# Cutting the opening weights of an MLP kernel into two rows by 131 KB and five rows by 328 KB

## The chip, the cores and the metric

The kernel runs on one core of a Trainium2 chip. The metric is the device time of one execution in microseconds; lower is better. The kernel before takes 398.3 us (the median of three executions, 397.71 to 398.58). Times inside an execution are counted from the start of the span that the profiler recorded.

## The reference

```python
y = _layernorm(x, axis=-1)                                  # x: 1 x 2048 x 1024, bf16
h = _gelu(jnp.einsum("bsd,df->bsf", y, w1) + b1)            # w1: 1024 x 3584
return jnp.einsum("bsf,fd->bsd", h, w2) + b2                # w2: 3584 x 1024
```

Each of the 2048 tokens is normalised over its 1024 channels, without gain or offset, then goes through a two-layer MLP with a hidden width of 3584 and the tanh form of GELU. All inputs and the output are bf16.

## The kernel before, in words

**Tiling.** Tokens come in 16 tiles of 128, and four tiles make a block of 512. The 1024 channels are 8 slices of 128 (`dt`), the 3584 hidden units are 28 rows of 128 (`r`). For each block the first product (`pe_row`, the matmul at L386) makes one row at a time: 8 matmuls of 128x128 weights against 512 tokens, summed in one PSUM bank, then GELU on ACT (L409). The second product (L451) takes all 28 rows of hidden units against w2, for 128 tokens and 512 output channels at a time; DVE adds b2 (L462) and SP stores.

**The opening.** The first block does not wait for whole weights. Its first seven rows (`R_WAVE = 7`, rows 0 to 6) are made in a wave of smaller matmuls, called cells here (`pe_wave`, L399), in an order that follows the loads:

1. Tiles 0 and 1 are turned by TensorE (`pe_T`, transposes at L342, copies out of PSUM by ACT at L358) as raw x, before they are normalised. Their cells run on raw values with 258 columns: 256 tokens and two columns of ones. DVE puts the normalisation in later, by subtracting the mean from the turned x (L511) for the rows to come and by fixing the seven rows in PSUM (L518, L521).
2. These 56 raw cells are ordered by `ROWS` (groups of rows), within a group by `QUARTERS` (two slices `dt` at a time), within a quarter by row and slice. With `ROWS = ((0, 1, 2, 3), (4, 5, 6))` a quarter of the first group is 8 cells, one of the second is 6.
3. After `T2_AT = 50` raw cells tile 2, which DVE and POOL have normalised by then (L255 statistics, L265, L262, L269), is turned into PSUM by eight transposes, and ACT copies it out.
4. Tile 2's 56 cells of 128 columns follow. After `T3_AT = 36` of them tile 3 is turned in the same way, then come the other 20, and then tile 3's own 56 cells, which wait for ACT's copy.
5. Rows 7 to 27 of block 0 follow as whole rows (L386).

Every engine works in its written order. PE therefore stands still at the first cell whose weights, tile or copy has not arrived, and everything behind that cell waits with it.

**The loads.** `dma` (L192) puts each load on SP's queue in a written order; each has its own semaphore. `SP_FIRST_LOADS` gives the first twelve: x0, x1, w0 to w3, x2, w4 to w7, x3 (b1 goes on ACT's queue). The rest of w1, the second block of x, w2, b2 and the last two blocks of x follow. `w0` to `w7` are entries of `w1_chunks`: each is a quarter (two slices `dt`) by 512 columns (four rows of hidden units), 256 rows of 1024 bytes in memory, 262 KB. w0 to w3 hold rows 0 to 3, w4 to w7 rows 4 to 7. w8 holds rows 8 to 11 with all slices, 1.05 MB in rows of 1024 bytes; w9 and w10 eight rows each in rows of 2048 bytes. A tile of x is 128 rows of 2048 bytes, also 262 KB. `pe_wave` and `pe_row` look up with `w1_chunk_of` which chunk a cell's weights are in, and wait for that chunk.

The functions that are touched follow.

Of the kernel before, what the change touches and what calls it, by code (L numbers as in the profile page):

```python
# [12 lines left out]
P = 128  # L13
# [10 lines left out]
GROUPS_0 = (0, 4, 8)  # L24
GROUPS_1 = (0, 8)
HALVES = (0, 4, 8)
ROWS = ((0, 1, 2, 3), (4, 5, 6))
QUARTERS = (0, 2, 4, 6, 8)
T2_AT = 50
T3_AT = 36  # L30
W1_EARLY = 2
W1_EARLY_COLS = 512
W1_COLS = (512, 1024, 1024)
N_W2_CHUNKS = 4
SP_FIRST_LOADS = ("x0", "x1", "w0", "w1", "w2", "w3", "x2", "w4", "w5", "w6", "w7", "x3")
ACT_FIRST_LOADS = ("b1",)
SLOT_0 = (1, 2, 3, 0)
N_ONES = 2
# [57 lines left out]
def bass_standalone__mixer_channel_mlp__prompt_kernel(  # L96
# [21 lines left out]
    R = R_WAVE  # L118
    assert R == NB1 + NB2 and R < FT
    assert NB1 + NB2 + 1 <= 8 and NB2 == 2  # L120
    assert all(c[-1] == DT for c in (GROUPS_0, GROUPS_1, HALVES))
    assert TPB == 4 and RAW == (0, 1) and sum(ROWS, ()) == tuple(range(R))

    w1_chunks = [(j0, j1, k * W1_EARLY_COLS, (k + 1) * W1_EARLY_COLS) for k in range(W1_EARLY)
                 for j0, j1 in zip(QUARTERS[:-1], QUARTERS[1:])]
    c0 = W1_EARLY * W1_EARLY_COLS
    for wdt in W1_COLS:
        w1_chunks.append((0, DT, c0, c0 + wdt))
        c0 += wdt
# [17 lines left out]
    with ExitStack() as es:  # L147
# [67 lines left out]
        def issue(item):  # L215
            if item == "b1":
                dma(b1r_sb[0:FT, :], b1.rearrange("(t p) -> t p", p=P), "b1", F * 2, waits=["b1z"])
            elif item[0] == "x":
                load_x_tile(int(item[1:]))
            elif item[0] == "w" and int(item[1:]) < len(w1_chunks):  # L220
                load_w1(int(item[1:]))
# [5 lines left out]
        dma_q[0] = sp  # L227
        for item in SP_FIRST_LOADS:
            issue(item)
# [312 lines left out]
        def wave_cell(r, dt, tiles, sig=None):  # L542
# [3 lines left out]

        cells = [(r, dt) for rows in ROWS for j0, j1 in zip(QUARTERS[:-1], QUARTERS[1:])
                 for r in rows for dt in range(j0, j1)]
# [5 lines left out]
        for j0, j1 in zip(HALVES[:-1], HALVES[1:]):  # L554
            for r in range(R):
                for dt in range(j0, j1):
                    if n == T3_AT:
                        pe_T(3, GROUPS_1, ("t",))
# [25 lines left out]
        for b in range(NB):  # L584
# [11 lines left out]
            for st in range(TPB):  # L596
                for dh in range(DH):
                    c0, c1 = dh * NCH, (dh + 1) * NCH
# [72 lines left out]
```

## Time and profile before

| | |
|---|---|
| median of three executions | 398.3 us (397.71 to 398.58) |
| the profiled execution | 398.81 us |
| its span | 397.6 us |
| the chain that ended last | PE 95% of the span |
| the first cell (L399) | at 6.2 us |
| tile 2's turn, tile 3's turn | at 12.2 and 15.9 us |
| the first whole row (L386) | at 20.8 us |
| DMA, 40 slices of 9.9 us | 252, 375, 387, 387, 387, 145 GB/s, then mostly under 30 |
| load to landing, eight pieces of 256 KB | median 5.5 us |

The profiled execution is 1.2 us longer than its span, which is the part outside of the recorded instructions. PE is the engine of all matmuls and PEld the weight loads that run ahead of them; DVE, ACT, POOL and SP are the vector, scalar, general-purpose and synchronising engines. A timeline line gives the start and the length in us, the engine, the line of the kernel and the operation with its output and input; the count at its end says how many were merged. Square brackets give the idle time of the engine just before and what ended it. In a chain of work that ended last each piece was released by the one above it. In a table by stretches the last two numbers are the mean busy share of the 16 DMA engines and what they moved in GB/s.

### The profile page before, as it was taken

The page shows a single profiled execution, that of the slowest core. Times are in us where ns is not written, and L with a number is a line of the kernel's source. Part 1 is how long each engine was busy: PE and PEld are TensorE (multiplying, and loading weights), DVE is VectorE, ACT ScalarE, POOL GpSimd, SP SyncE. Part 2 cuts the span into 40 slices and gives each one's busy share as a digit, 9 for nine tenths or more (in the row PEclk, how much of TensorE's full clock was granted, in tenths as well). Part 3 has the DMA queues.
Part 4 walks back from the last instruction along what each step waited for, and adds up shares of the span by engine and source line. Part 5 has one row for each costly group of instructions (what it writes and reads, how often), then busy time and mean ns, then how long its engine had stood idle before and what let it go on. Part 6 is the DMA issues. An engine that isn't in the chain of part 4 may idle for free.

```text
span 397.6 us, 4718 instructions
## 1 busy us (share of the span) xinstructions
PE 391.5 (98%) x2015; PEld 189.7 (48%) x2050; DVE 154.3 (39%) x335; ACT 82.7 (21%) x124; POOL 10.6 (3%) x56
## 2 busy tenths in 40 slices
PE   8999999999999999999999999999999999999998
PEld 7844444444444444444444444444444444444446
DVE  5759898989999005988100000001100000001111
ACT  3264430000134432000024433100003334400000
POOL 2101000020001000000000000000000000000000
DMA  7999930000000000000000000000000000000001
GB/s 252 375 387 387 387 145 15 26 26 16 26 1 2 0 0 2 26 14 28 26 15 0 0 2 0 12 16 26 13 28 13 2 0 0 2 13 26 15 26 28
DMA packets 16350, 23.64 MB, mean 59 GB/s; under 512 B 1482, under 2 KB 8522, under 8 KB 16330
## 3 DMA queue, kind: packets, MB, share of 16 engines
q1 hardware_dynamic: 16288, 23.33, 16.7%
q8 instruction: 16, 0.26, 0.3%
q14 instruction: 4, 0.03, 0.0%
q10 hardware_dynamic: 42, 0.01, 0.0%
HBM read 19.14 MB, written 4.19 MB: 59 GB/s over the span
## 4 chain that ended last, share of the span: by engine, by line
PE 95%; DMA 2%; SPq 1%; issue 1%; DVE 1%; POOL 0%
PE ps L451 48%; PE ps L386 45%; DMA x_sb<-in_x_dram 2%; SPq L192 1%; PE ps L399 1%; DVE st_sb L255 0%; PE ps_t L342 0%; POOL rstd_sb L262 0%; DVE x_sb L269 0%; DVE o_sb L462 0%; DVE mv_sb L265 0%
## 5 line engine op out<-in xcount | busy, mean ns | idle before, releaser
L451 PE MATMUL ps<-w_sb,hT_sb 128*128 128x512 bf16 (+1 forms) x964 | 193.4, 360 | 0.8
L386 PE MATMUL ps<-yT_sb,w_sb 128*128 128x512 bf16 x821 | 180.8, 379 | 1.0
L451 PEld LDWEIGHTS ps<-w_sb,hT_sb 128*128 128x128 bf16 x980 | 91.3, 98 | 102.6
L409 ACT ACTIVATE hT_sb<-ps,b_sb 128x512 bf16<-128x512 f32 x112 | 76.8, 688 | 253.2 <-PE ps L386 231.8
L386 PEld LDWEIGHTS ps<-yT_sb,w_sb 128*128 128x128 bf16 x840 | 82.1, 98 | 98.9
L462 DVE TENSOR_TENSOR o_sb<-ps,b_sb 128x512 bf16<-128x512 f32 (+1 forms) x35 | 22.6, 646 | 198.9 <-PE ps L451 198.9
L312 DVE STREAM_TRANSPOSE yT_sb<-x_sb 32x256 bf16<-32x256 bf16 x192 | 83.7, 436 | 26.4 <-PE ps L386 23.3
L255 DVE BATCH_NORM_STATS2 st_sb<-x_sb 128x6 f32<-128x512 bf16 x32 | 20.9, 671 | 7.3 <-DMA x_sb<-in_x_dram 7.3
L399 PE MATMUL ps<-yT_sb,w_sb 128*128 128x128 bf16 (+1 forms) x168 | 13.4, 237 | 1.4 <-DMA w_sb<-in_w_dram 1.4
L399 PEld LDWEIGHTS ps<-yT_sb,w_sb 128*128 128x128 bf16 x168 | 11.4, 98 | 3.1 <-DMA w_sb<-in_w_dram 2.2
L262 POOL TENSOR_TENSOR rstd_sb<-mv_sb,nhalf 128x1 f32<-128x1 f32 x14 | 7.7, 549 | 115.0 <-DVE mv_sb L265 115.0
L425 DVE TENSOR_TENSOR ps<-ps,row_r 128x256 f32<-128x256 f32 x21 | 8.9, 427 | 4.7 <-PE ps L386 4.7
L269 DVE TENSOR_SCALAR x_sb<-x_sb,mv_sb,rstd_sb 128x1024 bf16<-128x1024 bf16 x14 | 7.6, 544 | 3.3 <-POOL rstd_sb L262 2.7
L473 PE MATMUL ps<-const-bfloat16-1.0 128*128 128x128 bf16 x30 | 3.4, 300 | 0.8 <-PEq L656 0.8
L473 PEld LDWEIGHTS ps<-const-bfloat16-1.0 128*128 128x128 bf16 x30 | 3.0, 139 | 0.8 <-issue 0.8
L518 DVE SCALAR_TENSOR_TENSOR ps<-row_r,ncs,ps 128x256 f32<-128x256 f32 x7 | 3.4, 480 | 0.0
L265 DVE BATCH_NORM_AGGREGATE mv_sb<-st_sb 128x2 f32<-128x15 f32 x14 | 3.1, 222 | 0.4
L358 ACT COPY yT_sb<-ps_t 128x512 int32<-128x512 int32 (+1 forms) x3 | 1.5, 516 | 7.7 <-PE ps_t L342 7.7
L521 DVE TENSOR_TENSOR ps<-ps,row_r 128x256 f32<-128x256 f32 x7 | 3.0, 432 | 0.2
L490 ACT COPY row_r<-row_r 32x512 f32<-32x512 f32 x3 | 1.9, 617 | 3.2 <-DVE row_r L484 3.2
L511 DVE TENSOR_TENSOR yT_sb<-yT_sb,row_r 128x1024 bf16<-128x1024 bf16 x2 | 2.4, 1216 | 0.0
L342 PE MATMUL ps_t<-ident,x_sb 128*128 128x128 bf16 x20 | 1.7, 226 | 0.1
(21 smaller groups left out, 12.5 us busy)
## 6 DMA issues: line engine op xcount, KB each, us to landing
w_sb<-in_w_dram SPq DMA_DIRECT2D x4, 1792.0 KB, 18.3
w_sb<-in_w_dram SPq DMA_DIRECT2D x2, 2048.0 KB, 15.9
out_dram<-o_sb SPq DMA_DIRECT2D x31, 128.0 KB, 1.7
x_sb<-in_x_dram SPq DMA_DIRECT2D x3, 1024.0 KB, 14.3
w_sb<-in_w_dram SPq DMA_DIRECT2D x8, 256.0 KB, 5.5
x_sb<-in_x_dram SPq DMA_DIRECT2D x4, 256.0 KB, 4.2
w_sb<-in_w_dram SPq DMA_DIRECT2D x1, 1024.0 KB, 9.0
b_sb<-in_b_dram SPq DMA_DIRECT2D x1, 256.0 KB, 14.3
```

Source lines behind the costliest of these rows:

```text
L192: dma_q[0].op(lambda e, dst=dst, src=src: e.dma_start(dst, src), waits=waits, sig=sig, sem="d_" + sig, inc=16)
L255: return (lambda e, i=i, h=h, pw=pw: e.bn_stats(st_sb[i][:, 6 * h:6 * (h + 1)], x_sb[:, i, h * pw:(h + 1) * pw]), [x_ev[i][h if len(x_ev[i ...
L262: pool.op(lambda e, i=i, dst=dst, mv=mv: e.tensor_tensor(out=dst, in0=mv[:, 1:2], in1=nhalf[:, i:i + 1], op=ALU.pow), waits=[f"mv{i}", "nh ...
L269: return (lambda e, i=i, c0=c0, c1=c1: e.tensor_scalar(out=x_sb[:, i, c0:c1], in0=x_sb[:, i, c0:c1], scalar1=mv_sb[:, i, 0:1], scalar2=rst ...
L312: res.append((lambda e, src=src, dst=dst: e.transpose(out=dst, in_=src), waits, (f"tr{i}" if lastop else None), 0.47))
L386: pe.op(lambda e, b=b, r=r, dt=dt, bank=bank: e.matmul(unit_bank(bank)[:, 0:TB], lhsT=w1_sb[:, dt, r * P:(r + 1) * P], rhs=yT_sb[:, b % 2, ...
L399: pe.op(lambda e: e.matmul(unit_bank(bank)[:, n0:n1], lhsT=w1_sb[:, dt, r * P:(r + 1) * P], rhs=yT_sb[:, 0, dt, n0:n1], start=(dt == 0 and ...
L409: act.op(lambda e, r=r, n0=n0, n1=n1, bank=bank: e.activation(out=hT_sb[:, r, n0:n1], in_=unit_bank(bank)[:, n0:n1], func=ACT.Gelu_apprx_tanh,
L425: crit.append((est[sig], (lambda e, reg=reg: e.tensor_tensor(out=reg, in0=reg, in1=row_b(1), op=ALU.mult), [sig, "row_r"], ready, 0.45), 0))
L451: pe.op(lambda e, sl=sl, ft=ft, c0=c0, c1=c1, bank=bank: e.matmul(ps_2[:, bank, 0:c1 - c0], lhsT=hT_sb[:, ft, sl * P:(sl + 1) * P], rhs=w2 ...
L462: crit.append((est[sig], (lambda e, ob=ob, c0=c0, c1=c1, bank=bank: e.tensor_tensor(out=o_sb[:, ob, c0:c1], in0=ps_2[:, bank, 0:c1 - c0], ...
L473: pe.op(lambda e: e.matmul(ps_1[:, 0, 0:P], lhsT=ones, rhs=ones, start=True, stop=True))
```

## The change

The same weights are loaded in other pieces, and the raw cells are grouped to match. w0 to w3 hold rows 0 and 1 only: a quarter by 256 columns, 256 rows of 512 bytes, 131 KB each. w4 to w7 hold rows 2 to 6: a quarter by 640 columns, 256 rows of 1280 bytes, 328 KB each. w8 becomes 640 columns, rows 7 to 11, 1.31 MB in rows of 1280 bytes, and w9 and w10 stay. The raw cells come in the groups (0, 1) and (2 to 6), so a quarter of the first group is 4 cells and one of the second 10. x2 is issued behind w5 instead of behind w3. Tile 3 is turned after 44 cells of tile 2 instead of 36, which leaves 12 of them behind it. The number of loads and of matmuls stays as it is.

```diff
-ROWS = ((0, 1, 2, 3), (4, 5, 6))
+ROWS = ((0, 1), (2, 3, 4, 5, 6))
 QUARTERS = (0, 2, 4, 6, 8)
 T2_AT = 50
-T3_AT = 36
-W1_EARLY = 2
-W1_EARLY_COLS = 512
-W1_COLS = (512, 1024, 1024)
+T3_AT = 44
+W1_COLS = (640, 1024, 1024)
 N_W2_CHUNKS = 4
-SP_FIRST_LOADS = ("x0", "x1", "w0", "w1", "w2", "w3", "x2", "w4", "w5", "w6", "w7", "x3")
+SP_FIRST_LOADS = ("x0", "x1", "w0", "w1", "w2", "w3", "w4", "w5", "x2", "w6", "w7", "x3")
...
-    w1_chunks = [(j0, j1, k * W1_EARLY_COLS, (k + 1) * W1_EARLY_COLS) for k in range(W1_EARLY)
+    w1_chunks = [(j0, j1, rows[0] * P, (rows[-1] + 1) * P) for rows in ROWS
                  for j0, j1 in zip(QUARTERS[:-1], QUARTERS[1:])]
-    c0 = W1_EARLY * W1_EARLY_COLS
+    c0 = R * P
```

## The prediction

> **What bounds the kernel now.** I read the page first (span and the busy shares), then the chain that ended last, cut to its first 25 us, because the change touches nothing behind the opening; then the timeline of the opening, and last the stretches with their DMA rates. The page:
>
> ```profile
> span 397.6 us, 4718 instructions
> PE 391.5 (98%) x2015; PEld 189.7 (48%) x2050; DVE 154.3 (39%) x335; ACT 82.7 (21%) x124; POOL 10.6 (3%) x56
> ```
>
> PE is busy from end to end, so a microsecond is won or lost only where the opening moves the first full 512-column matmul (L386). The chain, start and length in us, shows what sets that moment:
>
> ```profile
> 6.36 6.71 DMA x_sb<-in_x_dram
> 13.09 1.30 DVE st_sb L255 x2
> ...
> 15.30 0.56 DVE x_sb L269
> 15.90 0.62 PE ps_t L342 x8
> 16.52 4.24 PE ps L399 x76
> ...
> 20.82 4.26 PE ps L386 x19
> ```
>
> Tile 3 of x lands at 13.09, is normalised by 15.86, turned by eight transposes from 15.90, and 76 cells of 128 columns follow with no hole. But the margin by which x3 is last is thin. In the timeline (start, length, engine, work; in brackets the idle time before and what ended it):
>
> ```profile
> 6.20 3.42 PEld L399 LDWEIGHTS ps<-yT_sb,w_sb 128*128 128x128 bf16 x32 [1.30 <-DMA w_sb<-in_w_dram]
> 9.01 1.28 DVE L255 BATCH_NORM_STATS2 st_sb<-x_sb 128x6 f32<-128x512 bf16 x2 [0.49 <-DMA x_sb<-in_x_dram]
> 10.16 0.55 PEld L399 LDWEIGHTS ps<-yT_sb,w_sb 128*128 128x128 bf16 x6 [0.54 <-DMA w_sb<-in_w_dram]
> 10.91 0.55 PEld L399 LDWEIGHTS ps<-yT_sb,w_sb 128*128 128x128 bf16 x6 [0.20 <-DMA w_sb<-in_w_dram]
> 11.67 0.55 PEld L399 LDWEIGHTS ps<-yT_sb,w_sb 128*128 128x128 bf16 x6 [0.20 <-DMA w_sb<-in_w_dram]
> 12.23 0.54 PEld L342 LDWEIGHTS ps_t<-ident,x_sb 128*128 128x128 bf16 x8
> 13.62 2.01 PEld L399 LDWEIGHTS ps<-yT_sb,w_sb 128*128 128x128 bf16 x36 [0.30 <-ACT yT_sb L358]
> 15.89 0.45 PEld L342 LDWEIGHTS ps_t<-ident,x_sb 128*128 128x128 bf16 x8 [0.26 <-DVE x_sb L269]
> 16.30 4.28 PEld L399 LDWEIGHTS ps<-yT_sb,w_sb 128*128 128x128 bf16 x76
> ```
>
> PE opens on w0 at 6.20, waits for w4, w5 and w6 (10.16, 10.91, 11.67), turns tile 2 at 12.23, runs 36 cells of tile 2 and then waits 0.26 us for tile 3. So the weights' landings set tile 2's turn, and tile 3's landing wins over that chain by only 0.26 us. The stretches (length, busy time of PE, PEld, DVE, ACT, POOL, then granted clock, DMA share, GB/s):
>
> ```profile
> 3.40:4.50 1.10, 1.10 (x17) 1.00 (x15) 1.08 (x2) 0.33 (x2) 0.00 (x0) 1.00 0.80 194
> 4.50:6.20 1.70, 0.58 (x11) 0.40 (x8) 1.70 (x6) 0.87 (x4) 0.10 (x1) 1.00 0.95 318
> 6.20:8.30 2.10, 2.09 (x19) 1.88 (x20) 1.77 (x9) 0.00 (x0) 0.97 (x2) 1.00 1.02 322
> 13.20:14.20 1.00, 0.98 (x15) 0.69 (x14) 1.00 (x2) 0.37 (x1) 0.00 (x0) 1.00 1.11 351
> 20.00:30.00 10.00, 9.95 (x57) 4.91 (x56) 5.56 (x14) 6.62 (x10) 0.00 (x0) 1.00 1.05 387
> ```
>
> Between 13.2 and 14.2 only w8 moves (rows of 1 KB), from 20 on only rows of 2 KB: that prices a row. At 3.4 to 4.5, where x gives way to the weights, the rate is only 194, and it stays at 318 to 322 up to 8.3.
>
> **The price of a row.** 351 GB/s on 16 DMA engines is 21.9 each, 46.7 ns for 1 KB; 387 is 24.2 each, 84.7 ns for 2 KB. A line through both: 8.7 ns a row and 38.0 ns for 1024 bytes. So 512 bytes cost 27.7 ns, 1280 bytes 56.2. Every one of the eight pieces keeps 256 rows, 16 for each engine: 0.75 us for the old pieces (the waits above end 0.75 and 0.76 apart, as they should), 0.44 for the new w0 to w3, 0.90 for the new w4 to w7. No row of 512 bytes is in the trace. From below it can't beat the line by more than the 8.7 ns (bytes alone, 19 ns); from above it costs as much as the 1 KB row, 46.7. I take the line, since it also fits the 1 KB rows' 0.75 us in the opening; the upper end is the first rival. The Trainium skill ("DMA: Bandwidth & Descriptors", section "Why small descriptors are slow (HBM only)") gives three cycles of overhead beside 32-byte beats, so 19 cycles for 512 bytes against 35 for 1 KB and 43 for 1280. As an estimate from that page the rows take 25.3 and 57.4 ns, tile 2's turn comes 0.09 us sooner than below and the sum is 398.4; no run here shows a row of that size yet.
>
> **The landings.** w0 to w3 lose 0.305 us each, 1.22 together; w4 to w7 gain 0.152 each. Times before are the releases above.
> - w0: 6.20 - 0.30 = 5.90. PE is free for it: its three filler matmuls start at 4.75 and ACT's last copy of tile 1 ends at 5.37.
> - x2 moves behind w4 and w5: 9.01 - 1.22 + 2 x 0.90 = 9.59. On SP it is issued two places later (each issue takes 0.43 to 0.60 us), at about 4.7 instead of 3.71, nearly 5 us ahead of its landing, so the issue hides under the queue; w4 and w5 go out two and one places sooner, w6, w7 and x3 where they were.
> - w6: 11.65 - 1.22 + 3 x 0.152 = 10.89. w7 (issued at 5.85, 6.5 us to landing, 12.4): 12.4 - 1.22 + 0.61 = 11.8. x3: 13.09 - 0.61 = 12.48.
> - w8 grows by 0.26 MB, just what the eight pieces lose (row 7 moves over). Its 64 rows per engine cost 0.61 more, so it lands where it did, at 7.04 + 9.0 = 16.0; row 7 needs it at 20.8. Without that cover of 4.8 us each late microsecond would count in full. Later chunks and w2 are unmoved.
>
> **PE.** A 258-column cell takes 0.11 us (w0's 32 cells ran in 3.5 us without a hole), a 128-column one 0.0559 (76 in 4.25). Rows 0 and 1 are 4 cells a piece, rows 2 to 6 are 10. w0 to w3: 5.90 to 7.66 (w3 lands at 7.0). w4 lands at 7.9, its cells run to 9.0; w5's to 10.1; then a wait for w6, 10.9 to 12.0; four cells of w7 to 12.45, where tile 2's turn stands (after 50 cells in both kernels). Tile 2's y comes 2.76 us behind its landing (13.09 to 15.85 in tile 3's row; the same DVE, POOL, DVE steps): 9.59 + 2.76 = 12.35. So tile 2 is turned at 12.45 instead of 12.23: PE starts 0.3 us sooner but gets there no sooner, because w4 to w6 and x2 all have to land first. The 1.39 us from the turn to the first tile 2 cell (12.23 to 13.62; six RAW cells and ACT's copy) stay. The 44 cells ahead of tile 3's turn take 2.46: 12.45 + 1.39 + 2.46 = 16.30. Tile 3's y is there at 12.48 + 2.81 = 15.29, a microsecond early, so the wait of 0.26 is gone, and x3's gain is lost on PE's backlog. Behind the turn (0.41) stand now only 12 cells (0.67) instead of 20 (1.12) to cover the copy, which releases tile 3's cells 1.30 behind the turn (15.89 to 17.19: copy at 16.56, 0.59 long): a new wait of 0.22, on which all of PE is queued. Then 56 cells, 3.13. End: 16.30 + 1.30 + 3.13 = 20.73 against 16.30 + 4.25 = 20.55 before: **0.18 us later**. DVE's centring of tiles 0 and 1 follows tile 3's y, so it ends earlier than its 18.11 and hides; so do its fixes, which follow tile 3's cells.
>
> **Sum.** Profiled execution 398.81 (span 397.6 and 1.2 around it) + 0.18 = 398.99. It stands 0.51 above the median of 398.3, so 398.5 for the median.
>
> **Rivals.**
> - *The small rows cost as much as the old ones* (slower). w0 to w3 then gain nothing and w4 to w7 cost 0.152 each: w6 lands at 12.11, tile 2 is turned at 13.66, the end is 1.21 later than forecast: 399.7. It decides (0.8 us over before) from 37 ns a row: (0.8 - 0.18) / 64 rows = 9.7 ns over 27.7. For it: the four pieces move just in the stretch where the engines are at 194 to 322 GB/s, so rows and their latency limit there, not bytes. Against it: the steady line. The Trainium skill (same page, section "Measured (HBM→SBUF, 128 partitions, SWDGE, issued from GpSimd)") has a rule against such pieces: batch to 1 MiB, small transfers go by descriptors. The 256 KB pieces ran at 91% of the best rate here, which speaks against it; for 131 KB nothing does yet.
> - *The slow start shrinks with the pieces* (faster). x1 lands at 1.22 + 3.0 = 4.2 and w0 at 6.20: 2.0 us for a piece worth 0.75. I left the excess of 1.2 in place. If all of it went, w6 and x2 would land 1.2 sooner, tile 2 would be turned at about 11.25 and PE reach tile 3's turn at 15.1 with y3 at 14.1: end 19.53, 397.3. Over half a microsecond more than half of that excess must go (0.98 us) for a gain of 0.8. Against it: the DMA count and rows are the same, and the gap lies at the change from x to weights, which stays.
> - *x3 still decides*, as the chain has it now, with the 0.61 us that it gains: turn at 15.29, end 15.29 + 1.30 + 3.13 = 19.72, 397.5. It needs tile 2's turn by 11.44, a microsecond sooner than worked out.
>
> **How the numbers follow.** About 0.2% (0.8 us) is what a measurement of this kernel can tell from no change. Forecast, within that: 0.50. Small rows dear, or stalls of the start that cost more with x2 queued behind six pieces: 0.36. The two faster ones: 0.14 together, since both need the slow start to shrink. The unshown row price and the stall are far larger than my 0.18. The range runs from 397.7 (a part of the excess gone) to 399.8 (small rows at the old price); the forecast's own range is 397.9 to 399.0.
>
> **What would show it.** PE's first cell at 5.9; waits for weights ahead of the fifth and the seventh piece; tile 2's statistics at 9.6 instead of 9.01; its turn at 12.45; no wait ahead of tile 3's turn at 16.3, but one of 0.2 for ACT's copy behind it; the first L386 matmul at 21.0 (20.82 + 0.18). The forecast is wrong if tile 2's turn lies outside 11.5 to 13.1, or if row 7 waits for w8.

## The result

The change makes the kernel slower. The median over seven executions is 399.44 us (399.12 to 400.67) against 398.37 us for the kernel before; the ratio is 1.0033, with a 95% interval of 1.0020 to 1.0045, so about 1.1 to 1.3 us. That lies in the forecast range, at its slower end. But the likeliest case, a shift within 0.2%, did not come.

The profiled execution of the kernel after took 400.67 us, 1.2 us over its own median, so it is not a typical one. The page:

```profile
span 399.2 us, 4753 instructions
PE 394.2 (99%) x2050; PEld 190.4 (48%) x2050; DVE 154.3 (39%) x335; ACT 82.8 (21%) x124; POOL 10.6 (3%) x56
```

PE is still the bound, and the span is 1.6 us longer. The chain that ended last, cut to the opening (start, length, work):

```profile
4.73 6.38 DMA x_sb<-in_x_dram
11.13 1.30 DVE st_sb L253 x2
...
13.34 0.56 DVE x_sb L267
13.95 0.62 PE ps_t L340 x8
14.57 0.66 PE ps L397 x6
15.24 2.63 PE ps L397 x44
17.88 0.46 PE ps_t L340 x8
18.36 0.59 ACT yT_sb L356
...
19.08 3.30 PE ps L397 x56
22.38 2.81 PE ps L384 x13
```

Line numbers are two lower than before. The x tile at its head is now x2 (issued at 4.73), not x3: tile 2 lands at 11.1, is turned at 13.95, and everything behind is PE's own work plus ACT's copy behind tile 3's turn. Weight loads of the same opening in the timeline (start, length, engine, work, idle time before and what ended it):

```profile
5.80 1.67 PEld L397 LDWEIGHTS ps<-yT_sb,w_sb 128*128 128x128 bf16 x16 [0.18 <-issue]
9.62 2.09 PEld L397 LDWEIGHTS ps<-yT_sb,w_sb 128*128 128x128 bf16 x20 [2.15 <-DMA w_sb<-in_w_dram]
12.05 1.43 PEld L397 LDWEIGHTS ps<-yT_sb,w_sb 128*128 128x128 bf16 x14 [0.34 <-DMA w_sb<-in_w_dram]
13.94 0.45 PEld L340 LDWEIGHTS ps_t<-ident,x_sb 128*128 128x128 bf16 x8 [0.46 <-DVE x_sb L267]
15.24 2.46 PEld L397 LDWEIGHTS ps<-yT_sb,w_sb 128*128 128x128 bf16 x44 [0.30 <-ACT yT_sb L356]
17.66 0.49 PEld L340 LDWEIGHTS ps_t<-ident,x_sb 128*128 128x128 bf16 x8
19.07 3.13 PEld L397 LDWEIGHTS ps<-yT_sb,w_sb 128*128 128x128 bf16 x56 [0.26 <-ACT ncs L562]
```

PE begins on time (5.80, worked out as 5.90) and finishes the 16 cells of rows 0 and 1. Then it stands still for 2.15 us: w4 comes at 9.62, and I had worked out 7.9. The stretch from 4.5 to 9.1 us shows that the loads come more slowly. The kernel before (length, busy times of PE, PEld, DVE, ACT, POOL, granted clock, DMA share, GB/s):

```profile
4.50:9.10 4.60, 3.47 (x38) 2.98 (x36) 3.78 (x15) 1.42 (x5) 1.07 (x2) 1.00 1.00 324
```

The same stretch of the kernel after:

```profile
4.50:9.10 4.60, 3.22 (x30) 2.61 (x27) 3.89 (x14) 1.69 (x5) 1.07 (x2) 1.00 0.95 288
```

The opening moves 36 GB/s less. The experiments ask why. "Over before" is always the ratio with its interval, times 398.5 us.

### The profile page after: what moved, and what is told of

It is laid out like the page before. It is cut to its first block, busy times and chain, and to the rows that moved or that the text cites. A ratio compares the mean times of both kernels' runs of the same rounds, so it can differ in the third digit from the quotient of the medians.

```text
span 399.2 us, 4753 instructions
## 1 busy us (share of the span) xinstructions
PE 394.2 (99%) x2050; PEld 190.4 (48%) x2050; DVE 154.3 (39%) x335; ACT 82.8 (21%) x124; POOL 10.6 (3%) x56
## 4 chain that ended last, share of the span: by engine, by line
PE 96%; DMA 2%; SPq 1%; DVE 1%; issue 0%; ACT 0%; POOL 0%
PE ps L449 49%; PE ps L384 45%; PE ps L397 2%; DMA x_sb<-in_x_dram 2%; SPq L190 1%; DVE st_sb L253 0%; PE ps_t L340 0%; ACT yT_sb L356 0%; POOL rstd_sb L260 0%; DVE x_sb L267 0%; DVE o_sb L460 0%; DVE mv_sb L263 0%; ACT ncs L562 0%
```

## Experiments: which part of the change costs

**The cut alone.** The kernel after, with x2 and tile 3's turn put back:

```diff
-T3_AT = 44
+T3_AT = 36
-SP_FIRST_LOADS = ("x0", "x1", "w0", "w1", "w2", "w3", "w4", "w5", "x2", "w6", "w7", "x3")
+SP_FIRST_LOADS = ("x0", "x1", "w0", "w1", "w2", "w3", "x2", "w4", "w5", "w6", "w7", "x3")
```

> Edit: the kernel after with x2 back behind w3 and tile 3's turn back after 36 cells, so only the cut of the weights differs from before. Theory A (the cut costs: w4 to w6 land later than the thinner w0 to w3 give back, PE stands still for them): most of the 1.07 us stays, 0.5 to 1.1 us over before. Theory B (x2 behind w5 is the cost: its statistics start late and tile 2's turn waits for its y): about 0, within 0.3 us of before. Theory C (tile 3's turn is too late and the copy behind it is uncovered): 0.25 us less than the kernel after.

Measured: ratio 1.0033 (1.0019 to 1.0047), 1.3 us over before: all of the loss, even a little above what theory A gave. Its weight loads in the timeline:

```profile
6.74 0.78 PEld L397 LDWEIGHTS ps<-yT_sb,w_sb 128*128 128x128 bf16 x8 [0.45 <-DMA w_sb<-in_w_dram]
9.57 3.63 PEld L397 LDWEIGHTS ps<-yT_sb,w_sb 128*128 128x128 bf16 x34 [2.05 <-DMA w_sb<-in_w_dram]
13.22 0.54 PEld L340 LDWEIGHTS ps_t<-ident,x_sb 128*128 128x128 bf16 x8
```

PE waits 0.45 us within rows 0 and 1, and then 2.05 us for w4. From 9.57 on it runs 34 cells of 0.107 us without a hole, and tile 2's turn is late because PE is. x2 was ready long before. So theory A holds for the part, though not yet for the reason. Theories B and C are not needed for the loss: it is all there without x2's and tile 3's move.

**x2 alone.** The kernel before with x2 behind w5:

```diff
-SP_FIRST_LOADS = ("x0", "x1", "w0", "w1", "w2", "w3", "x2", "w4", "w5", "w6", "w7", "x3")
+SP_FIRST_LOADS = ("x0", "x1", "w0", "w1", "w2", "w3", "w4", "w5", "x2", "w6", "w7", "x3")
```

> Edit: the kernel before with x2 behind w5 and nothing else. Two pieces of 0.75 us ahead of it put x2 at about 10.5 instead of 9.01, its y at 13.3, and tile 2's turn from 12.23 to 13.3. Theory B: 0.8 us over before (13.3 + 1.39 + 2.01 + 0.41 + 4.25 = 21.36 against 20.55). Theory A: x2 is not what decides, w6 is; under 0.3 us over before.

Measured: ratio 1.0028 (1.0017 to 1.0038), 1.1 us over before. The timeline:

```profile
6.31 5.61 PEld L399 LDWEIGHTS ps<-yT_sb,w_sb 128*128 128x128 bf16 x50 [0.69 <-DMA w_sb<-in_w_dram]
10.48 1.29 DVE L255 BATCH_NORM_STATS2 st_sb<-x_sb 128x6 f32<-128x512 bf16 x2 [1.97 <-DMA x_sb<-in_x_dram]
13.29 0.45 PEld L342 LDWEIGHTS ps_t<-ident,x_sb 128*128 128x128 bf16 x8 [1.37 <-DVE x_sb L269]
```

All as theory B worked it out (x2 at 10.5, the turn at 13.3), and a little dearer in time. So moving x2 is bad by itself too, but the two costs do not add: together with the cut they give 1.0031 to 1.0033, no more than the cut alone. Tile 2's turn waits for the later of PE's backlog and tile 2's y, and in the change both are late.

**Tile 3's turn alone.** The kernel before with `T3_AT = 44`:

> Edit: the kernel before with tile 3's turn after 44 cells instead of 36. By theories A and B the wait of 0.26 us ahead of the turn goes and one of 0.22 behind it comes: within 0.1 us of before. Theory C: 0.2 us or more over before.

Measured: ratio 1.0001 (0.9992 to 1.0010). As worked out, one wait replaces another: in its profile PE waits for nothing ahead of the turn and 0.26 us behind it, where before it waited 0.26 ahead. Theory C falls.

**The kernel after again**, with a profile of its own:

> The kernel after unchanged, with a profile of its own. In the first profile w4 lands at 9.6 us though 7.9 was worked out. If that is one late DMA engine by chance (theory D), w4's release moves by over half a microsecond from profile to profile and the time with it; if it belongs to the pieces of 1280-byte rows (theory A), PE's second wait ends near 9.6 again. The time: 1.0 to 1.1 us over before in both cases.

Measured: ratio 1.0031 (1.0021 to 1.0040). Its weight loads:

```profile
5.77 1.67 PEld L397 LDWEIGHTS ps<-yT_sb,w_sb 128*128 128x128 bf16 x16 [0.41 <-issue]
8.22 0.99 PEld L397 LDWEIGHTS ps<-yT_sb,w_sb 128*128 128x128 bf16 x10 [0.78 <-DMA w_sb<-in_w_dram]
9.90 0.99 PEld L397 LDWEIGHTS ps<-yT_sb,w_sb 128*128 128x128 bf16 x10 [0.69 <-DMA w_sb<-in_w_dram]
11.45 1.44 PEld L397 LDWEIGHTS ps<-yT_sb,w_sb 128*128 128x128 bf16 x14 [0.56 <-DMA w_sb<-in_w_dram]
13.38 0.45 PEld L340 LDWEIGHTS ps_t<-ident,x_sb 128*128 128x128 bf16 x8 [0.50 <-DVE x_sb L267]
```

w4 came 1.4 us sooner than in the first profile (8.22), so that much was chance, as theory D has it. The trace holds a landing for each of the 16 DMA engines: in the first profile 15 of them had brought their share of w4 by 7.30 and the last one at 9.57, and PE waited for that one. But it is still later than 7.9, w6 is 0.56 late (10.89 worked out), and tile 2's turn stands at 13.38 instead of 12.45: 0.93 late, where the time is about 1 us late. The rate from 4.5 to 9.1 is 281 GB/s here and 282 in the run of the cut alone. Something systematic remains.

## Experiments: why the cut pieces come slowly

**Other cuts.** Three groupings ask whether the length of the rows does it. In the first two the cut is by `ROWS`, with x2 and tile 3's turn as before:

```diff
-ROWS = ((0, 1), (2, 3, 4, 5, 6))
+ROWS = ((0, 1, 2), (3, 4, 5, 6))
...
```

> Edit: the cut alone (x2 behind w3, tile 3's turn after 36 cells), but rows 0 to 2 in w0 to w3 (768-byte rows) and rows 3 to 6 in w4 to w7 (1024-byte rows). Theory P (a row costs its steady price from the start, only profiles by chance showed stalls): w6 0.6 us sooner, tile 3's turn 0.35 us sooner than before: 0.35 us under before. Theory S (in the first 9 us the engines don't reach the steady rate with the shorter rows, so thin first pieces gain little, and the fuller second pieces hand PE more cells behind w6): between before and the cut (2, 5), 0.2 to 0.9 us over before.

Measured: ratio 1.0002 (0.9993 to 1.0011). Neither theory: worse than P's 0.35 us under before, better than S's 0.2 us over. The rate from 4.5 to 9.1 is 337 GB/s, so the pieces of 197 KB do not have the trouble of those of 131 KB.

```diff
-ROWS = ((0, 1), (2, 3, 4, 5, 6))
+ROWS = ((0, 1, 2, 3), (4, 5, 6))
...
```

> Edit: rows 0 to 3 in w0 to w3 as before, rows 4 to 6 in w4 to w7 (768-byte rows, 197 KB), row 7 moves to w8; x2 and tile 3's turn as before. This takes from the cut only that row 7 is no longer loaded ahead of x3. Theory P: w4 to w7 land 0.15 us sooner each, x3 0.61: 0.6 us under before. Theory S: the first pieces are as before, the short rows come between 8 and 11 us where the rate is nearly steady: 0.3 to 0.6 us under before. If any row under 1 KB is dear (theory R, 47 ns a row whatever its length): no gain, within 0.1 us of before.

Measured: ratio 0.9993 (0.9984 to 1.0002): 0.3 us under before by the middle, not clear of no change. In its profile x3 comes about a microsecond sooner than in the profile of before (12.11 against 13.09). Short rows late in the opening do no harm, which speaks against theory R but doesn't refute it.

In the third, the kernel before gets the 1280-byte rows only in w4 to w7:

```diff
-W1_EARLY = 2
-W1_EARLY_COLS = 512
-W1_COLS = (512, 1024, 1024)
+W1_EARLY_COLS = ((0, 512), (512, 1152))
+W1_COLS = (384, 1024, 1024)
...
```

> Edit: the kernel before with w4 to w7 at 640 columns (1280-byte rows, rows 4 to 8) and w8 at 384; the cells and their order stay. Theory P and theory S: w4 to w7 land 0.15 us later each, x3 0.61 later, tile 3's turn waits for it: 0.6 us over before. Theory L (it is the 1280-byte rows that stall an engine): another 0.7 us or more, 1.3 us over before, and a spread of the landings of one piece over the 16 engines of 1.2 us and more.

Measured: ratio 1.0019 (1.0010 to 1.0028), 0.8 us over before, where P and S gave 0.6 and L 1.3. The interval still reaches 1.1 us, but the rate does not fall:

```profile
4.50:9.10 4.60, 4.60 (x43) 4.04 (x41) 4.24 (x16) 1.49 (x5) 1.08 (x2) 1.00 1.07 366
```

The extra bytes ahead of x3 cost what they should, within the interval. The rows of 1280 bytes stall nothing here: the 16 engines land a piece of them within 0.8 us of each other, where theory L asked for 1.2 and more. Theory L falls.

**The pace of the issues.** SP puts out one load in about 0.5 us, whether it is of 131, 262 or 328 KB: with 131 KB pieces that is 257 GB/s. Two edits of the cut alone keep all rows and bytes and change only the issuing. The cut alone moves in the stretch from 4.5 to 9.1:

```profile
4.50:9.10 4.60, 2.75 (x28) 1.89 (x25) 4.25 (x16) 1.63 (x5) 1.07 (x2) 1.00 0.90 282
```

In the first edit, two pieces go by ACT's queue:

```diff
-SP_FIRST_LOADS = ("x0", "x1", "w0", "w1", "w2", "w3", "x2", "w4", "w5", "w6", "w7", "x3")
-ACT_FIRST_LOADS = ("b1",)
+SP_FIRST_LOADS = ("x0", "x1", "w0", "w2", "x2", "w4", "w5", "w6", "w7", "x3")
+ACT_FIRST_LOADS = ("b1", "w1", "w3")
```

> Edit: the cut alone with w1 and w3 issued on ACT's queue (behind b1) instead of SP's, so everything behind them is issued up to 1 us sooner. Theory I (the pieces are too small for SP's pace of one issue in 0.51 us, 257 GB/s with 131 KB, and engines run dry): the rate between 4.5 and 6.2 us rises to 300 GB/s and more, and the time falls by 0.5 us or more against the cut alone. Theory S without the pace: within 0.2 us of the cut alone, 1.1 to 1.5 us over before.

Measured: ratio 1.0012 (1.0003 to 1.0021), 0.5 us over before and 0.8 under the cut alone, although w0 now shares the engines with w1 and PE opens only at 6.52. From 4.5 to 6.2 the rate is 300 GB/s, as theory I asked for; from 4.5 to 9.1:

```profile
4.50:9.10 4.60, 3.47 (x31) 2.71 (x30) 4.24 (x15) 1.75 (x5) 1.07 (x2) 1.00 1.03 336
```

In the second, rows 0 and 1 come in two pieces of four slices, two issues fewer with the same 512-byte rows (`SP_FIRST_LOADS` names the pieces anew in the same order, which is left out):

```diff
-                 for j0, j1 in zip(QUARTERS[:-1], QUARTERS[1:])]
+                 for j0, j1 in zip(*((HALVES[:-1], HALVES[1:]) if rows == ROWS[0] else (QUARTERS[:-1], QUARTERS[1:])))]
...
```

> Edit: the cut alone with rows 0 and 1 in two pieces of four slices (262 KB, 512 rows of 512 bytes) instead of four of two slices; the same rows and bytes by two issues fewer. Theory I (SP's pace of one issue in 0.51 us feeds 131 KB pieces too slowly): the rate between 4.5 and 6.2 us rises to 290 GB/s or more (205 to 270 with four pieces), and the time falls by 0.5 us or more against the cut alone, to 0.2 to 0.8 us over before. Theory S (the 512-byte rows themselves are slow there): the rate stays under 270 and the time within 0.3 us of the cut alone, 1.0 to 1.5 us over before.

Measured: ratio 1.0005 (0.9996 to 1.0014), 0.2 us over before: 1.1 of the 1.3 us are gone. From its timeline, SP's issues of the two pieces (start, length):

```profile
1.69 0.97 SPq L190 DMA_DIRECT2D w_sb<-in_w_dram  x2
```

Its stretch from 4.5 to 9.1:

```profile
4.50:9.10 4.60, 2.66 (x28) 2.02 (x26) 4.25 (x15) 1.41 (x5) 1.07 (x2) 1.00 0.98 326
```

Two issues of 512 rows take 0.97, no more than two of 256 rows (the four of before took 1.97). One number missed: from 4.5 to 6.2 alone the rate was 278, not over 290; the recovery lies behind, where w4 to w7 were issued a microsecond sooner.

The last run turns it round. The kernel before, with its 1024-byte rows, gets rows 0 to 3 in eight pieces of 131 KB (the new names in `SP_FIRST_LOADS` are left out; the order stays):

```diff
+EIGHTHS = (0, 1, 2, 3, 4, 5, 6, 7, 8)
...
-                 for j0, j1 in zip(QUARTERS[:-1], QUARTERS[1:])]
+                 for j0, j1 in zip(*((EIGHTHS[:-1], EIGHTHS[1:]) if k == 0 else (QUARTERS[:-1], QUARTERS[1:])))]
```

> Edit: the kernel before with rows 0 to 3 in eight pieces of one slice (131 KB, 128 rows of 1024 bytes) instead of four of two slices; rows, bytes and order stay, four issues more on SP ahead of x2. Theory I (the pace of issues: 131 KB in 0.51 us is 257 GB/s): between 4.5 and 6.2 us the rate falls from 318 to 339 below 290 GB/s, and everything behind lands 0.3 to 0.5 us later: 0.3 to 0.6 us over before. Theory S (only the 512-byte rows are slow there): the rate stays over 310 and the time within 0.15 us of before.

Measured: ratio 1.0036 (1.0023 to 1.0050), 1.4 us over before, with no short row in it and the cells in the order of before. The stretch from 4.5 to 9.1:

```profile
4.50:9.10 4.60, 3.98 (x40) 3.21 (x39) 3.82 (x14) 1.55 (x5) 1.07 (x2) 1.00 0.93 273
```

Its waits in the timeline, for the last of the eight pieces, for x2 and for the next quarter:

```profile
8.93 0.66 PEld L400 LDWEIGHTS ps<-yT_sb,w_sb 128*128 128x128 bf16 x7 [0.63 <-DMA w_sb<-in_w_dram]
9.57 1.29 DVE L256 BATCH_NORM_STATS2 st_sb<-x_sb 128x6 f32<-128x512 bf16 x2 [0.92 <-DMA x_sb<-in_x_dram]
10.86 0.56 PEld L400 LDWEIGHTS ps<-yT_sb,w_sb 128*128 128x128 bf16 x6 [1.27 <-DMA w_sb<-in_w_dram]
```

So the rows are not it, and theory S falls in the form that blames them. What the kernels whose rate falls share is pieces of 131 KB issued one behind another on one queue. Theory I missed two numbers here. The rate from 4.5 to 6.2 is 291, not under 290; the fall lies from 6.2 to 8.3, at 231. And the loss is more than twice the 0.3 to 0.6 us that it gave.

The profile also gives the time from a load's issue to its landing. For the eight pieces of the kernel before (w0 to w7) and then the eight of 131 KB (the profile counts a KB as 1024 bytes; the last number is the median in us):

```profile
w_sb<-in_w_dram SPq DMA_DIRECT2D x8, 256.0 KB, 5.5
w_sb<-in_w_dram SPq DMA_DIRECT2D x8, 128.0 KB, 3.4
```

Before, this time grows from 4.5 us for w0 to 6.5 for w7: issued loads pile up ahead of the engines. In the eighths it stays at 3.2 to 3.5 us from the second piece to the seventh, and these land 0.48 us apart on average, which is the pace at which SP issues them. Nothing piles up there, as theory I says. This speaks against a rival that the run with two queues can't exclude, a price that each load pays in its queue behind the issue: if that were longer than an issue, the loads would pile up.

| kernel | first pieces, on one queue unless said | GB/s, 4.5 to 9.1 | ratio to before |
|---|---|---|---|
| before | 4 of 262 KB, rows of 1024 B | 324 | 1 |
| tile 3's turn alone; rows 4 and 3 | 4 of 262 KB, rows of 1024 B | 362; 327 | 1.0001; 0.9993 |
| x2 alone; 1280-byte rows in w4 to w7 | 4 of 262 KB, rows of 1024 B | 332; 366 | 1.0028; 1.0019 |
| after; again | 4 of 131 KB, rows of 512 B | 288; 281 | 1.0033; 1.0031 |
| the cut alone | 4 of 131 KB, rows of 512 B | 282 | 1.0033 |
| before in eighths | 8 of 131 KB, rows of 1024 B | 273 | 1.0036 |
| cut, two queues | 4 of 131 KB, rows of 512 B, two by ACT | 336 | 1.0012 |
| cut in halves | 2 of 262 KB, rows of 512 B | 326 | 1.0005 |
| rows 3 and 4 | 4 of 197 KB, rows of 768 B | 337 | 1.0002 |

x2 alone and the 1280-byte rows lose time at a full rate: they put more bytes ahead of x2 or x3.

**Looking for a better version.** Two edits of the kernel with rows 0 to 3 and 4 to 6: x1 by ACT's queue, or x2 behind w2.

```diff
-SP_FIRST_LOADS = ("x0", "x1", "w0", "w1", "w2", "w3", "x2", "w4", "w5", "w6", "w7", "x3")
-ACT_FIRST_LOADS = ("b1",)
+SP_FIRST_LOADS = ("x0", "w0", "w1", "w2", "w3", "x2", "w4", "w5", "w6", "w7", "x3")
+ACT_FIRST_LOADS = ("x1", "b1")
```

> Edit: rows 4 to 6 in w4 to w7 (row 7 in w8, as in the run with rows 0 to 3 and 4 to 6), and x1 issued on ACT's queue ahead of b1, so every load behind it on SP's is issued 0.5 us sooner. By theory I the dip at 3.4 to 4.5 us (about 200 GB/s in most profiles) fills up and all landings come 0.2 to 0.5 us sooner: 0.4 to 0.9 us under before. If that dip has nothing to do with the pace of issues: 0.2 to 0.4 us under before, like the run without this edit.

Measured: ratio 0.9994 (0.9985 to 1.0003). The stretch from 3.4 to 4.5 fills up to 361 GB/s, but x0 and x1 share the engines, so tile 0's statistics start at 4.01 and PE opens at 6.19, against 3.52 and 5.70 without the edit; no gain over that run.

```diff
-SP_FIRST_LOADS = ("x0", "x1", "w0", "w1", "w2", "w3", "x2", "w4", "w5", "w6", "w7", "x3")
+SP_FIRST_LOADS = ("x0", "x1", "w0", "w1", "w2", "x2", "w3", "w4", "w5", "w6", "w7", "x3")
```

> Edit: the same weights, and x2 issued behind w2 instead of behind w3. Tile 2's turn waited 0.29 us for its y there; x2 lands 0.7 us sooner, w3 0.67 later, which PE's backlog of 258-column cells covers. Tile 2's turn then follows w6, 0.2 to 0.3 us sooner; tile 3's turn comes to wait for x3 instead, so 0.0 to 0.2 us less than the run without this edit, 0.3 to 0.5 us under before.

Measured: ratio 0.9996 (0.9987 to 1.0005). Tile 2's turn did not wait for its y any more, but its profile has a low rate at the start (142 GB/s from 3.4 to 4.5) and PE opens only at 6.33. None of the three is clear of the kernel before.

## Why the prediction was right or wrong

**The direction and the range held; the likeliest case did not.** The sum gave 0.18 us later, measured are about 1.1 to 1.3 us, which belongs to the slower case (0.36).

**The step that failed** is in the landings: "each issue takes 0.43 to 0.60 us ... so the issue hides under the queue", and with it pieces priced by their rows alone. The price of a row is not what failed: other cuts with short rows keep the rate, and 1024-byte rows lose it in pieces of 131 KB. The pieces' share in the pace of SP's issues was the term that I set to nothing. Three edits that change only issues or pieces and leave the length of the rows moved the time by 0.8 and 1.1 us down and 1.4 up. In the second profile of the kernel after, w6 is 0.56 and x2 about 1.0 late (10.58 against 9.59), and tile 2's turn 0.93.

**The pace is not all of that lateness.** As an estimate, four pieces at 0.51 us for an issue instead of the 0.44 worked out make 0.3 us. The rest shows in the landings of the single DMA engines, as a wait ends with the last of the 16. In that profile the middle engine brought x2 at 8.99, against 8.41 before: 0.58 later, just what the prediction had. w6 came at 10.12 by the middle engine, 0.26 later than the prediction's shift of 0.76 from the 10.62 of before. But the last engine brought x2 1.57 behind the middle one, against 0.58 before. These are single profiles. The sums shifted all landings alike and had no term for engines that drift apart. No run tests whether the thin pieces make them drift or chance does: the last and the first engine's landings of w6 are 1.8 to 2.7 us apart in the three profiles with this cut on one queue, 1.4 in the profile of before and 0.5 in that of tile 3's turn alone, but also 1.7 in the halves, which lose next to nothing.

**x2's place** was worked out right as a mechanism (y2 some 2.8 us behind the landing, then the turn). It sets the turn in both profiles of the kernel after, with waits of 0.46 and 0.50, and costs 1.1 us alone. I had it 0.1 us ahead of being late, with 9.59 as landing; with the real landing it decides.

**PE's steps** behind the turn held: 1.30 from the turn to the first tile 2 cell (1.39 worked out), 2.42 for 44 cells (2.46), the new wait behind tile 3's turn (0.26; 0.22 worked out), 3.13 for the last 56 cells. PE did start at 5.8. That x3's gain would be lost on PE's backlog held too: tile 3's turn waits for nothing.

**The rivals.** The slower one came nearest in time (399.7 against 399.44), but its mechanism, 512-byte rows as dear as 1024-byte ones, is not what the eighths and the halves show: there the loss comes and goes with the pieces, at unchanged rows. So its nearness in time is luck. The chance of 0.36 also covered stalls of the start, which is nearer to what the runs show, but no price was worked out for them. The rule to batch transfers into larger ones, which I cited beside it from the Trainium skill ("DMA: Bandwidth & Descriptors", section "Measured (HBM→SBUF, 128 partitions, SWDGE, issued from GpSimd)"), points the right way. The traces agree: at the same row length the kernel with 131 KB pieces moved 273 GB/s and the one with 262 KB pieces 324. The two faster rivals did not happen.

**What stays open.** The pace alone does not explain every number. In the eighths the loss is 1.4 us where the pace gave 0.3 to 0.6, and the busy share of the engines falls from 1.00 to 0.93 where the rate falls by 16%, so they also moved fewer bytes while busy. There the rate is still down between 9.1 and 11.0 us (267 and 245 GB/s), when the 131 KB pieces have passed and 262 KB pieces move that were issued three microseconds earlier; and the halves' rate rose later than expected. That issuing sooner, or in fewer pieces, takes back most of the loss is shown: 0.8 and 1.1 of 1.3 us. Why engines drift apart was not resolved, nor why a single one brought w4 so late in one profile.

## What to carry to other kernels

Work out a piece's bytes over the time of its issue, and compare that with the rate of the engines: here 131 KB in 0.51 us is 257 GB/s, under the 324 to 366 that the opening otherwise moves, so thinner first pieces bought an earlier start and lost the landings behind. Look also at the last DMA engine of a load, not only at the mean rate: the wait ends with it. A head start of PE is worth nothing when the next gate (the sixth weight piece, a tile's statistics) doesn't move with it; follow the sum to the last gate, and price the issue queue as a resource of its own.

## What the runs showed of the hardware

- An issue on SP's queue took 0.38 to 0.51 us in most cases for 128, 256 or 512 rows alike, from 131 to 328 KB; in this range its price goes by the load, not by its size. The 2.1 MB loads w9 and w10 took 2.3 and 3.0 us to issue in the kernel before.
- Pieces of 131 KB issued 0.48 us apart on one queue landed 3.2 to 3.5 us behind their issue without a backlog (the eighths); pieces of 262 KB fell behind from 4.5 to 6.5 us (before).
- A wait for a load ends with the last of the 16 DMA engines: in the first profile of the kernel after, 15 had landed w4 by 7.30, the last did at 9.57, and PE went on at 9.62.
- The opening differs much from execution to execution. Between 3.4 and 4.5 us the kernel before moved 194 GB/s, and the run that differs from it only in tile 3's turn, much later, 325. The landing of w4 differs by 1.4 us between the two profiles of the kernel after. A single profile of the first 10 us carries about a microsecond of chance.
- Rows of 512, 768, 1024 and 1280 bytes could be used without a loss of rate in the opening (324 to 366 GB/s), as long as pieces were of 197 KB or more or came by two queues.
